# Moving turned tokens inside SBUF, and gathering the rows of five chunks by six transfers: a fused convolution and feed-forward kernel on one Trainium2 core

## The chip, the core and the metric

The kernel runs on one core of a Trainium2 chip. The metric is the device time of one execution in microseconds (us); below it stands as the median of three runs. The engines are TensorE (PE for the matmuls, PEld for the weight loads), VectorE (DVE), ScalarE (ACT), GpSimd (POOL) and SyncE (SP). SP computes nothing here: it issues transfers (DMAs), in the order in which they stand in its queue. SBUF is the core's working memory with 128 partitions; PSUM takes the matmuls' sums; DRAM is the large memory outside.

## The reference, cut to what matters

```python
# x: (8, 4096, 192), weight_gen: (8, 4096, 8 heads, 7 taps), all float32
w = softmax(weight_gen, over the 7 taps)
x_pad = 6 zero rows in front of every sequence of x
conv[b, s, h, g] = sum_k w[b, s, h, k] * x_pad[b, s + k, h, g]     # 24 channels a head
h = conv.reshape(32768, 192) @ w_in          # w_in: (192, 2048)
r = relu(h)
out = (r * r) @ w_out                        # w_out: (2048, 192)
```

## The kernel before

**Tiles.** Partition `p` holds 256 consecutive tokens. The program walks 64 chunks `c` of 4 tokens a partition, so a chunk has 512 tokens (`N`). For a chunk DVE computes the softmax and the convolution, token on partition, into a tile `pr` of 128 x 4 x 192 (line 392 multiplies by a tap, line 405 adds). The first product needs the channels on partitions: `turn` brings the chunk into `xT` (128 partitions x 3 x 512). There the 192 channels are three groups `k` of 64, and both halves of the partitions hold the same three groups, since two matmuls of 64 rows run side by side. ACT rounds `xT` to the high part `xh` (line 435) and DVE takes the rest as low part `xl` (line 438): three instructions each for a chunk, one for each `k`.

**The turn before.** VectorE's transpose (line 497) turns blocks of 32 x 32 into a tile `xr`. Four transfers (line 503) write `xr` to a tile `xd` in DRAM, and two (line 508) read `xd` back, one into each half of `xT`. SP issues the reads when all four writes have landed.

**The steps.** A chunk is 8 steps `j`. In a step PE runs 18 matmuls of the first product for chunk `c` (line 532), then the second product of a step two behind (lines 613 to 623, or 648). ACT runs ReLU, square and the rounding to `gh` (lines 549, 556, 560), DVE the difference `gl` or `du` (lines 569, 572). All other work is hung into these steps by a table (`at(chunk, step, function)`): the turn for chunk m stands at step 2 of chunk m - 1 (most m), the high parts at its steps 5 and 6, the low parts at 6 and 7.

**Two kinds of chunk.** Chunks 6 to 62 are scaled (`is_scaled`): their second product runs partly in fp16, with factors that `measure` takes from a group's input (ACT, line 270, at step 2 of an even chunk, two chunks ahead). Chunks 1 to 5 are not, and 0 and 63 go paths of their own.

**The output of a chunk.** PE leaves the result channel-major. `sum_turned` adds the two halves of the sums into a tile `X`; the 64 last channels also need the other half of the partitions added. `store_turned` transposes `X` by blocks into `Y` (lines 676 and 680) and gathers the rows token-major into `o_sb`. A scaled chunk does that by six transfers (line 686) and is written a step group later (`close_scaled`, line 697). An unscaled chunk adds the other half by a transfer on SP (line 664) and a DVE addition (line 679), gathers by 24 transfers of 16 KB (line 690), and is written at once by four transfers (line 102).

**SP's queue.** The next input group, `wt` and `xt` (lines 156 and 157, two chunks' worth), is loaded at step 5 of odd chunks, and so stands in SP's queue behind what `store_turned` issued at steps 3 and 4.

Of the kernel before, what the change touches and what calls it, by code (L numbers as in the profile page):

```python
# [8 lines left out]
F32 = mybir.dt.float32  # L9
# [5 lines left out]
ALU = mybir.AluOpType  # L15
# [15 lines left out]
def kernel(  # L31
# [9 lines left out]
    nc = tc.nc  # L41
    B, S, D = x.shape
# [3 lines left out]
    P = 128  # L46
    Q = 32
    HALO = K - 1
    R = B * S // P
    PPB = S // R  # L50
    TC = 4
    NCH = n_chunks or R // TC
# [3 lines left out]
    D1 = 64  # L56
    ND = D // D1
    N = TC * P
# [3 lines left out]
    N_PE = 2  # L62
# [7 lines left out]
    FIRST = 6  # L70
    GL_POOL = 5
    SCALE_STEP = NJ
# [8 lines left out]
    op = ctx.enter_context(tc.tile_pool(name="op", bufs=1))  # L81
    dram = ctx.enter_context(tc.tile_pool(name="dram", bufs=2, space=bass.MemoryType.DRAM))
# [6 lines left out]
    def put_out(c, t0, t1, o_sb, reads):  # L89
        rows = slice(rows_of(c) + t0, rows_of(c) + t1)  # L90
        if reads == 0:
            nc.sync.dma_start(out=out.rearrange("(p r) d -> p r d", r=R)[:, rows, :], in_=o_sb[:, t0:t1])
            return
        if reads == 3:
            v = out.rearrange("(q a b r) d -> b q a r d", q=P // Q, a=P // Q, r=R)
            n = v.shape[0] // 4
            for k in range(4):
                nc.sync.dma_start(out=v[k * n:(k + 1) * n, :, :, rows, :], in_=o_sb[k * Q:(k + 1) * Q, t0:t1])
            return
        v = out.rearrange("(q a b r) d -> q b a r d", q=P // Q, a=2 ** reads, r=R)  # L100
        for q in range(P // Q):
            nc.sync.dma_start(out=v[q, :, :, rows, :], in_=o_sb[q * Q:(q + 1) * Q, t0:t1])
# [7 lines left out]
    def is_scaled(c):  # L110
        return FIRST <= c < NCH - 1
# [21 lines left out]
    def rows_of(c):  # L133
        return (c + CPG if c < CPG else c - CPG if c < 2 * CPG else c) * TC
# [144 lines left out]
    def factor(gi):  # L279
        f = att.tile([P, 1], F32, name="x_fac", bufs=2)  # L280
        x_out[gi] = fo = att.tile([P, 1], F32, name="x_out", bufs=3)
        nc.vector.tensor_tensor(out=f, in0=x_pow[gi], in1=v_unroot, op=ALU.mult)  # L282
        n = P // (P // Q) ** 2
        for b in range(n):
            nc.gpsimd.dma_start(out=fo[b * P // n:(b + 1) * P // n], in_=f[b::n])  # L285
# [48 lines left out]
    def conv_steps(c, on_pe, moving=False):  # L334
# [3 lines left out]
        n = TC * H  # L338
        wf = wt[:, lo:lo + TC].rearrange("p t h k -> p (t h) k")
        if c < N_PE:  # L340
            e = eps[c]
# [5 lines left out]
        parts = xts[c] = {}  # L347
# [26 lines left out]
        prs = {}  # L374
# [115 lines left out]
        def turn():  # L490
            xr = att.tile([P, D // Q, P], F32, name="xr")
            xT = att.tile([P, ND, N], F32, name="xT")
            for k in range(ND):
                src[k] = xT[:, k]
            pr = prs.pop(0).rearrange("p t (b i) -> p t b i", i=Q)
            if c < NCH - 1:
                nc.vector.transpose(xr.rearrange("p b (t j) -> p t b j", j=Q), pr)
            else:
                for t in range(TC):
                    nc.vector.transpose(xr[:, :, t * Q:(t + 1) * Q].rearrange("p b (i m) -> p b m i", i=2), pr[:, t])  # L500
            xd = dram.tile([D, N], F32, name="xd")
            for q in range(P // Q):
                nc.sync.dma_start(
                    out=xd[:, q * P:(q + 1) * P].rearrange("(b i) n -> i b n", i=Q),
                    in_=xr[q * Q:(q + 1) * Q],
                )
            for h in range(2):
                nc.sync.dma_start(out=xT[h * D1:(h + 1) * D1], in_=xd.rearrange("(k p) n -> p k n", p=D1))

        return steps + taps() + [turn], splits  # L510

# [140 lines left out]
    def sum_turned(c, parts=(1, 0)):  # L652
        acc = accs[c]
        if c not in works:
            works[c] = stage.tile([P, 3, N], F32, name="raw")
        X = works[c]
        for k in parts:
            nc.scalar.copy(X[:, k], acc[2 * k])  # L658
        for k in parts:
            nc.vector.tensor_tensor(out=X[:, k], in0=acc[2 * k + 1], in1=X[:, k], op=ALU.add)  # L660
        if 1 in parts and is_scaled(c):
            nc.gpsimd.dma_start(out=X[0:D1, 1], in_=X[D1:P, 1], accum_op=ALU.add)  # L662
        elif 1 in parts:
            nc.sync.dma_start(out=X[0:D1, 2], in_=X[D1:P, 1])

    def store_turned(c, part):
        X = works[c]

        def blocks(v):
            return v.rearrange("p (a t i) -> p t a i", a=P // Q, t=TC) if is_scaled(c) else v  # L670

        if part == 0:
            o_sb = op.tile([P, TC, D], F32, name="o_sb", bufs=2)
            Y = stage.tile([P, 2, N], F32, name="raw")
            outs[c] = o_sb, Y
            nc.vector.transpose(blocks(Y[:, 0]), X[:, 0])
        else:
            if not is_scaled(c):
                nc.vector.tensor_tensor(out=X[0:D1, 1], in0=X[0:D1, 1], in1=X[0:D1, 2], op=ALU.add)
            nc.vector.transpose(blocks(outs[c][1][0:D1, 1]), X[0:D1, 1])  # L680
        o_sb, Y = outs[c]
        y = Y[:, part].rearrange("p (t q i) -> p q t i" if c < N_PE or is_scaled(c) else "p (q t i) -> p q t i", t=TC, i=Q)
        for e in range(P // Q if part == 0 else D1 // Q):
            d0 = part * P + e * Q
            if is_scaled(c):
                nc.sync.dma_start(out=o_sb[:, :, d0:d0 + Q], in_=outs[c][1][e * Q:(e + 1) * Q, part])
                continue
            for q in range(P // Q):
                queue = nc.gpsimd if part and c == NCH - 2 else nc.sync
                queue.dma_start(  # L690
                    out=o_sb[q * Q:(q + 1) * Q, :, d0:d0 + Q],
                    in_=y[e * Q:(e + 1) * Q, q],
                )
        if part and not is_scaled(c):
            put_out(c, 0, TC, o_sb, 2)

    def close_scaled(c):
        o_sb, f = outs[c][0], x_out[c // CPG]
        nc.vector.tensor_scalar(out=o_sb, in0=o_sb, scalar1=f, scalar2=f, op0=ALU.mult, op1=ALU.mult)
        put_out(c, 0, TC, o_sb, 3)  # L700

    outs = {}
# [19 lines left out]
    def store(c, t0, t1):  # L722
        put_out(c, t0, t1, outs[c][0], 1 if c == 0 else 0)
# [115 lines left out]
    def at(c, j, f):  # L839
        todo.setdefault((c + j // NJ, j % NJ), []).append(f)  # L840
# [40 lines left out]
    for gi in range(FIRST // CPG, NCH // CPG):  # L881
        at(CPG * gi - 2, 2, lambda gi=gi: measure(gi))
        at(CPG * gi - 2, 3, lambda gi=gi: power(gi))
        at(CPG * gi, 2, lambda gi=gi: factor(gi))
    for c in range(FIRST, NCH - 2):
        at(c + 1, SCALE_STEP, lambda c=c: close_scaled(c))

    plan_conv(2, conv2[6:], split2)
    plan_conv(3, *conv_steps(3, 0, True))
# [8 lines left out]
    for c in range(1, NCH):  # L898
        tail = c == NCH - 1
        for j in range(NJ):  # L900
# [28 lines left out]
            if split_sum:  # L929
                for f in fs[:N_AHEAD]:  # L930
                    f()
                del fs[:N_AHEAD]
                sum_turned(done, (0,))
            elif done is not None:
                sum_turned(done)
            if split_sum:
                highs_of(c, fbs)
                sum_turned(done, (1,))
            for f in fs:
                f()  # L940
            if c > 1:
                for part in range(2):
                    if j == (LOAD_STEP if tail else 2 * part + 2 if is_scaled(c - 1) else OUT_STEP + part):
                        store_turned(c - 1, part)
# [7 lines left out]
    c = NCH - 1  # L952
# [15 lines left out]
    t, end = TC - 1, range(NF - 4, NF)  # L968
# [6 lines left out]
    o_sb, tmp = outs[c]  # L975
# [33 lines left out]
```

## Time and profile before

| | |
|---|---|
| median of 3 runs | 2075.03 us (2075.01 to 2076.12) |
| the profiled execution's own time | 2076.22 us |
| span of its instructions | 2074.1 us, 1.00 of the full TensorE clock granted on average (0.998) |
| PE busy | 2054.8 us (99%) |
| DVE busy | 1873.6 us (90%) |
| ACT busy | 1840.6 us (89%) |
| POOL busy | 222.2 us (11%) |
| share of the chain that ended last | PE 84%, ACT 5%, DMA 3%, DVE 3% |
| transfers: hardware queue | 300280 packets, 181.04 MB, 37.6% of 16 engines |

The table is read so: the profiled execution's time lies 2.1 us over its span, and 1.2 us over the median. PE is nearly always busy, so the question for any change is what makes PE wait in the 1% that is left, and what makes its matmuls run at a lower clock.

### The profile page before, as it was taken

Reading aid. Unit: us, or ns where it says so; the run is one execution under the profiler, and the core shown is the slowest. Engines: PE = TensorE matmul, PEld = TensorE weight load, DVE = VectorE, ACT = ScalarE, POOL = GpSimd, SP = SyncE. Lnnn points to the kernel's source line nnn. Section 1 sums busy time; section 2 is a strip of 40 time slices with the busy share of each in tenths; the row PEclk is TensorE's granted clock in tenths of the full one; section 3 lists DMA queues with packets and bytes.
Section 4 is the critical chain, followed back from the end, with each engine's and each line's share of the span. In section 5 each row is a group of like instructions: output and inputs, shape, how many; then the busy total and the mean of one; then the engine's idle time right before and its main releaser. Section 6 shows DMA issues by size and latency. Waiting matters only on the chain.

```text
span 2074.1 us, 49551 instructions
## 1 busy us (share of the span) xinstructions
PE 2054.8 (99%) x19484; PEld 1621.0 (78%) x19484; DVE 1873.6 (90%) x2953; ACT 1840.6 (89%) x3551; POOL 222.2 (11%) x366
## 2 busy tenths in 40 slices
PE   9999999999999999999999999999999999999999
PEld 8898877777777777777777777777777777777778
DVE  8998989999999989999899998999989989999985
ACT  8988988989989989889898898998888988889986
POOL 0000110111110111101111101111011111011110
PEclk9999999999999999999999999999999999999999
DMA  8434454544544535545345454455453553544532
GB/s 233 95 64 100 109 123 97 119 84 100 122 106 107 120 66 117 117 101 119 74 108 125 98 113 92 94 119 115 100 118 72 112 127 95 114 86 100 121 61 56
DMA packets 322081, 217.78 MB, mean 105 GB/s; under 512 B 215584, under 2 KB 272928, under 8 KB 318008
## 3 DMA queue, kind: packets, MB, share of 16 engines
q1 hardware_dynamic: 300280, 181.04, 37.6%
q0 software_dynamic: 21568, 33.59, 9.6%
q8 instruction: 152, 2.49, 0.5%
q14 instruction: 81, 0.66, 0.1%
HBM read 106.52 MB, written 49.55 MB: 75 GB/s over the span
## 4 chain that ended last, share of the span: by engine, by line
PE 84%; ACT 5%; DMA 3%; DVE 3%; issue 1%; SPq 1%; POOL 0%; ACTq 0%; DVEq 0%; POOLq 0%
PE ph L532 42%; PE acc L613 25%; PE acc L617 9%; PE acc L623 5%; PE acc L648 3%; DMA xT<-xd 2%; ACT gh L560 1%; ACT rg L549 1%; ACT rg L556 1%; SPq L690 1%; PE acc L590 1%; DVE du L569 1%; DMA xt<-in_x_dram 1%; DMA pr<-pr 0%; ACT du L270 0%
## 5 line engine op out<-in xcount | busy, mean ns | idle before, releaser
L532 PE MATMUL ph<-xh,W 64*128 64x512 f32 x6096 | 909.5, 403 | 0.1
L549 ACT ACTIVATE rg<-ph 128x512 f32<-128x512 f32 x992 | 539.7, 598 | 174.3 <-PE ph L532 172.1
L532 PEld LDWEIGHTS ph<-xh,W 64*128 64x128 f32 x6096 | 578.5, 186 | 135.6 <-ACT gh L560 23.4
L613 PE MATMUL acc<-gh,V 64*128 64x512 f32 x5472 | 666.7, 376 | 0.0
L556 ACT ACTIVATE rg<-rg 128x512 f32<-128x512 f32 x1007 | 581.6, 636 | 0.2
L560 ACT CAST gh<-rg 128x512 fp32r<-128x512 f32 x1008 | 576.8, 628 | 3.0 <-PE acc L590 3.0
L613 PEld LDWEIGHTS acc<-gh,V 64*128 64x128 f32 x5472 | 519.6, 186 | 72.5 <-ACT gh L560 0.2
L532 PE MATMUL ph<-xl,W 64*128 64x512 f32 x3048 | 418.1, 377 | 9.7 <-DVE xl L438 9.3
L569 DVE TENSOR_TENSOR gl<-rg,gh 128x512 f16<-128x512 f32 x570 | 391.1, 742 | 31.7 <-ACT gh L560 31.7
L392 DVE TENSOR_TENSOR pr<-xt,wt 128x768 f32<-128x768 f32 x440 | 412.6, 950 | 2.5 <-DMA pr<-pr 0.2
L532 PEld LDWEIGHTS ph<-xl,W 64*128 64x128 f32 x3048 | 291.5, 186 | 54.7 <-DVE xl L438 15.0
L405 DVE TENSOR_TENSOR pr<-pr 128x768 f32<-128x768 f32 x309 | 294.8, 954 | 4.2
L569 DVE TENSOR_TENSOR du<-rg,gh 128x512 f16<-128x512 f32 x342 | 231.8, 732 | 48.6 <-ACT gh L560 48.4
L617 PE MATMUL acc<-gl,du 64*128 64x512 f16 x1140 | 173.4, 381 | 0.3 <-DVE gl L569 0.2
L662 POOL DMA_DIRECT2D raw<-raw x57 | 47.4, 831 | 1154.0 <-DVE raw L660 874.9
L660 DVE TENSOR_TENSOR raw<-acc,raw 128x512 f32<-128x512 f32 x124 | 85.3, 691 | 72.4 <-ACT raw L658 71.7
L617 PEld LDWEIGHTS <-du 64*128 64x128 f16 x1824 | 53.6, 95 | 109.9 <-issue 109.5
L435 ACT CAST xh<-xT 128x512 fp32r<-128x512 f32 x186 | 108.4, 619 | 26.1 <-DMA xT<-xd 25.9
L438 DVE TENSOR_TENSOR xl<-xT,xh 128x512 fp32r<-128x512 f32 x186 | 121.0, 681 | 2.3 <-ACT xh L435 2.3
L285 POOL DMA_DIRECT2D x_out<-x_fac x232 | 112.4, 494 | 85.6 <-DVE x_fac L282 82.2
L410 POOL DMA_DIRECT2D pr<-pr x63 | 56.7, 900 | 504.1 <-DVE pr L392 459.5
L617 PE MATMUL acc<-du 64*128 64x512 f16 x684 | 103.7, 382 | 0.0
(131 smaller groups left out, 1239.6 us busy)
## 6 DMA issues: line engine op xcount, KB each, us to landing
xT<-xd SPq DMA_DIRECT2D x124, 384.0 KB
xt<-in_x_dram SPq DMA_DIRECT2D x30, 1344.0 KB
out_dram<-o_sb SPq DMA_DIRECT2D x254, 96.0 KB
pr<-pr POOLq DMA_DIRECT2D x63, 384.0 KB, 5.9
xd<-xr SPq DMA_DIRECT2D x248, 96.0 KB
o_sb<-raw SPq DMA_DIRECT2D x342, 64.0 KB
raw<-raw POOLq DMA_DIRECT2D x57, 128.0 KB, 4.3
wt<-in_weight_gen_dram SPq DMA_DIRECT2D x31, 224.0 KB
```

The source lines that it names most:

```text
L285: nc.gpsimd.dma_start(out=fo[b * P // n:(b + 1) * P // n], in_=f[b::n])
L392: tt(out=dst, in0=src, in1=wf[:, t0 * H:t1 * H, k:k + 1].broadcast_to([P, m, G]), op=ALU.mult)
L405: tt(out=prs[k0], in0=prs[k0], in1=prs.pop(k), op=ALU.add)
L435: nc.scalar.copy(parts["h"][:, k, n], src[k][:, n])
L438: tt(out=parts["l"][:, k, n], in0=src[k][:, n], in1=parts["h"][:, k, n].bitcast(F32), op=ALU.subtract)
L532: nc.tensor.matmul(two[i], w, order(xx[rows, k]), start=(n == 0), stop=(n == last))
L549: nc.scalar.activation(r, ph, AF.Relu)
L556: nc.scalar.activation(r, r, AF.Square)
L560: nc.scalar.copy(gh, rgs[c, fb])
L569: nc.vector.tensor_tensor(out=gl, in0=g, in1=h, op=ALU.subtract)
L613: nc.tensor.matmul(acc[b + h], V[rows, fb, e:e + P], two_halves(g[rows]), start=fb == 0 and e < 2 * P, stop=False)
L617: nc.tensor.matmul(acc[h], V16[rows, 2 * j + i, 0:P], gls[c, j][rows, i], start=False, stop=last and i == 1)
```

## The change

`turn` no longer uses DRAM. The channels are taken in another order: two transposes, one for the even and one for the odd channels (`s`), each read `pr` with a step of two elements and write 384 contiguous elements. In `xr` a partition then holds what two neighbouring partitions of `xT` need, and eight transfers from SBUF to SBUF (for each quarter `q` of the source partitions, one into each half of `xT`) do the rest. `xT` is the same as before.

The unscaled chunks 1 to 5 take the path of the scaled ones: the other half is added by an accumulating transfer on POOL's queue, the transpose reads `X` in an order that leaves six gathers instead of 24, and `close` writes the chunk at step 0 of the chunk after (`at(c + 1, 8)`).

```diff
         if reads == 3: ...
+        if reads == 2:
+            v = out.rearrange("(q j r) d -> j q r d", q=P // Q, r=R)
+            n = Q // 4
+            for k in range(4):
+                nc.sync.dma_start(out=v[k * n:(k + 1) * n, :, rows, :], in_=o_sb[k * Q:(k + 1) * Q, t0:t1])
+            return
...
-            pr = prs.pop(0).rearrange("p t (b i) -> p t b i", i=Q)
+            pr = prs.pop(0).rearrange("p t (k i s) -> p s k t i", k=ND, s=2)
             if c < NCH - 1:
-                nc.vector.transpose(xr.rearrange("p b (t j) -> p t b j", j=Q), pr)
+                for s in range(2):
+                    nc.vector.transpose(xr[:, s * ND:(s + 1) * ND].rearrange("p k (t j) -> p k t j", j=Q), pr[:, s])
...
-            xd = dram.tile([D, N], F32, name="xd")
             for q in range(P // Q):
-                nc.sync.dma_start(
-                    out=xd[:, q * P:(q + 1) * P].rearrange("(b i) n -> i b n", i=Q),
-                    in_=xr[q * Q:(q + 1) * Q],
-                )
-            for h in range(2):
-                nc.sync.dma_start(out=xT[h * D1:(h + 1) * D1], in_=xd.rearrange("(k p) n -> p k n", p=D1))
+                for h in range(2):
+                    nc.sync.dma_start(out=xT[h * D1:(h + 1) * D1, :, q * P:(q + 1) * P], in_=xr[q * Q:(q + 1) * Q])
...
-        if 1 in parts and is_scaled(c):
+        if 1 in parts:
             nc.gpsimd.dma_start(out=X[0:D1, 1], in_=X[D1:P, 1], accum_op=ALU.add)
-        elif 1 in parts:
-            nc.sync.dma_start(out=X[0:D1, 2], in_=X[D1:P, 1])
...
+        x, y = X[0:n, part], Y[0:n, part]
+        if is_scaled(c):
+            nc.vector.transpose(y.rearrange("p (a t i) -> p t a i", a=P // Q, t=TC), x)
+        else:
+            y = y.rearrange("p (a t i) -> p t a i", a=P // Q, t=TC) if c < N_PE else y.rearrange("p (b i) -> p b i", i=Q)
+            nc.vector.transpose(y, x.rearrange("p (b m a) -> p b a m", a=4, m=Q // 4))
+        for e in range(n // Q):
             d0 = part * P + e * Q
-            for q in range(P // Q): ...
+            nc.sync.dma_start(out=o_sb[:, :, d0:d0 + Q], in_=Y[e * Q:(e + 1) * Q, part])
+
+    def close(c):
+        put_out(c, 0, TC, outs[c][0], 2)
...
-    for c in range(FIRST, NCH - 2):
-        at(c + 1, SCALE_STEP, lambda c=c: close_scaled(c))
+    for c in range(1, NCH - 2):
+        at(c + 1, SCALE_STEP, lambda c=c: (close_scaled if is_scaled(c) else close)(c))
```

On SP's queue this is what stands for chunks 2 to 4, before (`raw` is `X` or `Y`, an `x24` at the end counts transfers in a row):

```order
L664 DMA raw<-raw 64x512
L503 DMA xd<-xr 32x6x128 x4
L508 DMA xT<-xd 64x3x512 x2
L690 DMA o_sb<-raw 32x4x32 x24
L102 DMA out_dram<-o_sb 8x4x768 x4
L156 DMA wt<-in_weight_gen_dram 128x448
L157 DMA xt<-in_x_dram 128x2688
L664 DMA raw<-raw 64x512
```

And the same place now:

```order
L510 DMA xT<-xr 64x3x128 x8
L682 DMA o_sb<-raw 128x4x32 x6
L162 DMA wt<-in_weight_gen_dram 128x448
L163 DMA xt<-in_x_dram 128x2688
L104 DMA out_dram<-o_sb 8x4x768 x4
L510 DMA xT<-xr 64x3x128 x8
```

The input load now stands behind 8 + 6 transfers, no longer behind 4 + 2 + 24 + 4, and the chunk's four writes come after it.

On DVE at the turn of a scaled chunk, before (`raw` is the output's `Y` and `X`, `gl` the difference that the second product needs):

```order
L569 TENSOR_TENSOR gl<-rg,gh 128x2x256 x2
L282 TENSOR_TENSOR x_fac<-x_pow,coef 128x1
L497 STREAM_TRANSPOSE xr<-pr 128x4x6x32
L676 STREAM_TRANSPOSE raw<-raw 128x4x4x32
L569 TENSOR_TENSOR gl<-rg,gh 128x2x256 x2
```

And now:

```order
L571 TENSOR_TENSOR gl<-rg,gh 128x2x256 x2
L288 TENSOR_TENSOR x_fac<-x_pow,coef 128x1
L504 STREAM_TRANSPOSE xr<-pr 128x384 x2
L676 STREAM_TRANSPOSE raw<-raw 128x4x4x32
L571 TENSOR_TENSOR gl<-rg,gh 128x2x256 x2
```

One transpose of 768 elements a partition has become two of 384 in the same place; nothing else has moved there.

## Rows read from the trace of the kernel before

**Rows 1.** The page: busy time, share of the span and instructions of each engine.

```profile
PE 2054.8 (99%) x19484; PEld 1621.0 (78%) x19484; DVE 1873.6 (90%) x2953; ACT 1840.6 (89%) x3551; POOL 222.2 (11%) x366
```

**Rows 2.** Waits: who waited for whom, us in total, times, longest us.

```profile
ACT xh L435 <- DMA xT<-xd: 25.9, 34, 2.7
ACT du L270 <- DMA xt<-in_x_dram: 7.2, 2, 5.4
```

**Rows 3.** The chain that ended last: start us, us, what.

```profile
326.21 2.14 PE ph L532 x18
...
960.70 2.14 PE ph L532 x18
992.22 2.18 PE ph L532 x18
...
1025.40 2.14 PE ph L532 x18
...
2009.37 2.14 PE ph L532 x18
```

**Rows 4.** Timeline of a chunk whose turn is late: start us, us, engine, instructions [idle before].

```profile
997.38 1.83 SPq L503 DMA_DIRECT2D xd<-xr  x4
1002.66 1.30 SPq L508 DMA_DIRECT2D xT<-xd  x2
1009.77 1.14 ACT L435 CAST xh<-xT 128x512 fp32r<-128x512 f32 x2 [2.21 <-DMA xT<-xd]
```

**Rows 5.** Timeline of a chunk in which nobody waits for the turn.

```profile
1061.09 0.98 DVE L497 STREAM_TRANSPOSE xr<-pr 128x768 f32<-128x768 f32 x1
1062.10 1.81 SPq L503 DMA_DIRECT2D xd<-xr  x4
1063.50 1.39 DVE L569 TENSOR_TENSOR gl<-rg,gh 128x512 f16<-128x512 f32 x2 [0.83 <-ACT gh L560]
1065.73 1.29 SPq L508 DMA_DIRECT2D xT<-xd  x2
1072.24 1.15 ACT L435 CAST xh<-xT 128x512 fp32r<-128x512 f32 x2
```

**Rows 6.** DMA view of two stretches: packets, MB, share of 16 engines (1062 to 1065.8, 1002.6 to 1006.9).

```profile
q1 hardware_dynamic: 832, 0.39, 50.9%
...
q1 hardware_dynamic: 306, 0.59, 55.6%
```

**Rows 7.** Timeline of chunks 3 and 4: SP, ACT and PE.

```profile
139.08 16.75 SPq L690 DMA_DIRECT2D o_sb<-raw  x24
159.54 0.42 SPq L157 DMA_DIRECT2D xt<-in_x_dram  x1
166.61 1.48 ACT L270 ACTIVATE du<-xt 128x1536 bf16<-128x1536 f32 x1 [5.38 <-DMA xt<-in_x_dram]
156.97 0.83 PE L532 MATMUL ph<-xh,W 64*128 64x512 f32 x6
161.07 0.83 PE L532 MATMUL ph<-xh,W 64*128 64x512 f32 x6
174.77 0.81 PE L532 MATMUL ph<-xh,W 64*128 64x512 f32 x6
```

**Rows 8.** Busy time of the engines from 170 to 174.5; behind POOL the granted clock.

```profile
170.00:174.50 4.50, 3.95 (x18) 3.01 (x20) 4.00 (x11) 4.50 (x10) 0.00 (x0) 0.62 0.50 108
```

**Rows 9.** Timeline of chunk 6: ACT and PE.

```profile
234.92 1.49 ACT L270 ACTIVATE du<-xt 128x1536 bf16<-128x1536 f32 x1 [1.83 <-DMA xt<-in_x_dram]
254.76 0.48 PE L532 MATMUL ph<-xl,W 64*128 64x512 f32 x2 [2.07 <-DVE xl L438]
```

**Rows 10.** Groups by line, shapes kept apart: count | busy us, mean ns | idle before.

```profile
L497 DVE STREAM_TRANSPOSE xr<-pr 128x768 f32<-128x768 f32 x61 | 59.5, 975 | 0.1
L500 DVE STREAM_TRANSPOSE xr<-pr 128x192 f32<-128x192 f32 x4 | 1.5, 499 | 0.0
L226 DVE SCALAR_TENSOR_TENSOR du<-raw,du 128x384 uint32<-128x384 uint32 x16 | 8.6, 554 | 0.0
```

More of the change, by code (lines that the diff above doesn't have):

```diff
@@ L494, in turn @@
                 src[k] = xT[:, k]
-            pr = prs.pop(0).rearrange("p t (b i) -> p t b i", i=Q)
+            pr = prs.pop(0).rearrange("p t (k i s) -> p s k t i", k=ND, s=2)
             if c < NCH - 1:
-                nc.vector.transpose(xr.rearrange("p b (t j) -> p t b j", j=Q), pr)
+                for s in range(2):
+                    nc.vector.transpose(xr[:, s * ND:(s + 1) * ND].rearrange("p k (t j) -> p k t j", j=Q), pr[:, s])
             else:
                 for t in range(TC):
-                    nc.vector.transpose(xr[:, :, t * Q:(t + 1) * Q].rearrange("p b (i m) -> p b m i", i=2), pr[:, t])
-            xd = dram.tile([D, N], F32, name="xd")
+                    nc.vector.transpose(xr[:, :, t * Q:(t + 1) * Q].rearrange("p b (i m) -> p b m i", i=2), pr[:, :, :, t])
             for q in range(P // Q):
-                nc.sync.dma_start(
-                    out=xd[:, q * P:(q + 1) * P].rearrange("(b i) n -> i b n", i=Q),
-                    in_=xr[q * Q:(q + 1) * Q],
-                )
-            for h in range(2):
-                nc.sync.dma_start(out=xT[h * D1:(h + 1) * D1], in_=xd.rearrange("(k p) n -> p k n", p=D1))
+                for h in range(2):
+                    nc.sync.dma_start(out=xT[h * D1:(h + 1) * D1, :, q * P:(q + 1) * P], in_=xr[q * Q:(q + 1) * Q])
         return steps + taps() + [turn], splits
@@ L660, in sum_turned @@
             nc.vector.tensor_tensor(out=X[:, k], in0=acc[2 * k + 1], in1=X[:, k], op=ALU.add)
-        if 1 in parts and is_scaled(c):
+        if 1 in parts:
             nc.gpsimd.dma_start(out=X[0:D1, 1], in_=X[D1:P, 1], accum_op=ALU.add)
-        elif 1 in parts:
-            nc.sync.dma_start(out=X[0:D1, 2], in_=X[D1:P, 1])
     def store_turned(c, part):
         X = works[c]
-        def blocks(v):
-            return v.rearrange("p (a t i) -> p t a i", a=P // Q, t=TC) if is_scaled(c) else v
+        n = D1 if part else P
         if part == 0:
@@ L675, in store_turned @@
             outs[c] = o_sb, Y
-            nc.vector.transpose(blocks(Y[:, 0]), X[:, 0])
-        else:
[L678 to L683, printed above, removed]
-            d0 = part * P + e * Q
[L685 to L695, printed above, removed]
+        o_sb, Y = outs[c]
+        x, y = X[0:n, part], Y[0:n, part]
+        if is_scaled(c):
+            nc.vector.transpose(y.rearrange("p (a t i) -> p t a i", a=P // Q, t=TC), x)
+        else:
+            y = y.rearrange("p (a t i) -> p t a i", a=P // Q, t=TC) if c < N_PE else y.rearrange("p (b i) -> p b i", i=Q)
+            nc.vector.transpose(y, x.rearrange("p (b m a) -> p b a m", a=4, m=Q // 4))
+        for e in range(n // Q):
+            d0 = part * P + e * Q
+            nc.sync.dma_start(out=o_sb[:, :, d0:d0 + Q], in_=Y[e * Q:(e + 1) * Q, part])
+    def close(c):
+        put_out(c, 0, TC, outs[c][0], 2)
     def close_scaled(c):
```

## The prediction, on record before the changed kernel ran

> **What bounds the kernel now.** I read the page first: PE is busy for 2054.8 us, 99% of the span [rows 1], so only what makes PE wait or run slowly can be won. Next, who waited for whom. Two waits for transfers stand out, both on ACT: 34 times, 25.9 us in all and 2.7 us at the longest, for `xT`, the turned tokens, and twice, 7.2 us in all, for the input load `xt` [rows 2].
>
> What they cost PE is read from the chain that ended last [rows 3]. The 18 matmuls that begin a chunk's last step recur at 960.70 and 992.22, which makes an undisturbed chunk 31.52 us, and then at 1025.40, which makes the next 33.18. From 326.21 to 2009.37 are 53 chunks: 1683.16 us, where 53 x 31.52 is 1670.56. **In the steady part 12.6 us are lost**, and all else there is PE at its own pace.
>
> Why the chunk before 1025.40 lost 1.66 is in its timeline [rows 4]. SP issued the four writes to `xd` at 997.38, could issue the reads only at 1002.66, and ACT sat idle for 2.21 us until `xT` landed at 1009.77. So about 0.55 us of such a wait is absorbed and the rest goes to PE. The undisturbed chunk [rows 5] shows how near that always is: the transpose ended at 1062.07 (1061.09 + 0.98), and ACT took `xT` at 1072.24 without waiting. ACT therefore wants `xT` **10.17 us after the transpose**; in the late chunk it came 12.4 us after SP could begin.
>
> The early part loses in another way [rows 7]. In chunk 3 SP spends 16.75 us on 24 gathers, from 139.08, then writes the chunk, and issues the load of `xt` only at 159.54. ACT needs it for `measure` and idles 5.38 us until 166.61. PE's first-product groups start at 156.97 and 161.07, 4.10 us for a step; the one two steps on starts at 174.77, 13.70 us later where 8.20 are due: 5.5 us lost. That is more than a wait, since after PE's idle stretch the granted clock was 0.62 on average from 170 to 174.5 [rows 8], part of it at the lower of the two levels, 1.2 GHz instead of 2.4. In chunk 6 the same load is 1.83 us late, and PE later idles 2.07 us for a low part `xl` that DVE, set back with ACT, brings late [rows 9].
>
> **The turn, part by part.** Removed: four writes to DRAM, the wait for them, two reads. Added: eight transfers of 96 KB, 64 x 3 runs of 512 bytes each, and one transpose more.
>
> When will `xT` land? Issue first. Before, four transfers of the same 192 runs took 1.81 us of SP, a pitch of 0.45, and SP saw the last of them landed at 1065.73, which is 3.63 us after the first issue and 2.27 after the fourth one's (1062.10 + 3 x 0.45) [rows 5]. Eight at that pitch land 7 x 0.45 + 2.27 = 5.4 us after the transpose. If each takes as long to issue as a read does (1.29 / 2 = 0.65 us), it is 6.8. Then the data. The packets of the writes were 832, all but 64 of 512 bytes, with 50.9% of 16 engines over 3.8 us: 37 ns each. Eight transfers have 1536 such packets, 3.6 us on 16 engines, which hides under the issuing. No row shows a plain 512-byte packet from SBUF to SBUF; the upper bound is a 2 KB packet from DRAM, 55.6% of 16 engines over 4.3 us for 306, so 125 ns [rows 6], and with it the data alone take 12 us. I take 37 ns, the same size and source, and so a landing at 5.4 to 6.8 us. Now and then a transfer is held up: in the late chunk SP waited 5.28 us after the first issue instead of 3.63 [rows 4, 5]. With that 1.65 on top it is 8.5 at worst, still before 10.17. **All of the 12.6 us should go.** Behind the eight on SP stand the chunk's six gathers, which nobody needs before the next chunk; they could begin at 1067.02 (1065.73 + 1.29), 4.95 us after the transpose, and now can after eight issues, 3.6 to 5.2 us after it.
>
> The transposes. One of 768 elements took 975 ns; two of 384 that read with a step of two elements are not in the trace. From below they cost the same; an elementwise instruction that reads one operand with that step took 554 ns for 384 [rows 10], and two such are 1.11 us, 0.13 more. From above: the last chunk's transposes, which write with a long step, took 499 ns for 192 elements, 2.6 ns each, so 2.0 us and 1.02 more. I take 0.13, the row with the same step on the same side. What hides it is the 0.83 us for which DVE then waits for ACT's `gh` [rows 5]. At the upper bound 0.2 us would spill into a DVE that has no gap for the next 20 us, and the `xl` at its end would be 0.2 us later; PE would feel little of it. Cost: nothing, 0 to 0.2 us a chunk.
>
> The Trainium skill has a rule against this part. DMA: Bandwidth & Descriptors, section Rules for kernel authors, advises one large transfer instead of many small ones, and calls transfers to disjoint halves of the partitions not worth while because they share the same 16 engines. By that page's fit (section Anatomy of one DMA, about 2.0 us plus the bytes at 436 GB/s), eight in a row without overlap would be an estimated 17.8 us, and the change a loss. The trace disagrees on the overlap: four transfers landed within 3.63 us of the first issue [rows 5].
>
> **The output of chunks 1 to 5.** Removed: 24 gathers in favour of six, DVE's addition, SP's `raw` transfer. The load of `xt` now stands behind eight and six transfers; six at 0.70 (16.75 / 24) are 4.2 us, so at chunk 3 it leaves SP near 145 instead of 159.54, some 14 us earlier, more than the 5.38 it was late; likewise for the 1.83 at chunk 6. That returns 5.5 us and, by the gap alone, 2.07. The accumulating transfer goes to POOL, which is 11% busy [rows 1], steps ahead of its use. The ten transposes that read `X` with a step of four cost DVE between nothing and 0.7 us each (the 1.02 above, at 512 instead of 768 elements); the removed addition makes up for part of it, and PE's late `xl` in chunk 6 is the place where it could show.
>
> **The sum**, against the profiled execution's own 2076.2 us: 12.6 + 5.5 + 2.07 = 20.2 us, so 2056.0. That execution ran 1.2 us over the median of the runs, 2075.03, so for the median I predict **2055 us**, 1.0% faster.
>
> **Rivals.**
> - *Only the turn pays.* The early stalls stay, because something else is late next: ACT has much extra work in chunks 4 to 6, so that without the load's wait it may still set PE back, or the strided transposes keep DVE late. For it: PE's gap in chunk 6 was for DVE, not for the load. Against it: in chunk 4 the idle ACT waited for nothing but the load. Time: 2075.0 - 12.6 = 2062.4, with the half of it gone 2058.6.
> - *The wait is replaced.* `xT` comes early, but the third `xl` of a chunk is then held by DVE itself, which runs without a gap from 1063.50. Against it: undisturbed chunks run at 31.52 us with that same DVE. Time: within 2 us of 2075.
> - *Slower: the eight transfers do not overlap.* They land when the engines have worked off 1536 packets. At 125 ns that is 12 us of data and, with 1.6 us for first and last, 13.6; ACT then waits 3.4 us in each of some 60 chunks and PE loses 2.9: 170 us, a time near 2245. It turns into a loss as soon as they land about 10.7 us after the transpose. In a row without overlap, 8 x 2.27 = 18.2 us, it would be some 450. Against it: 37 ns for the same size, and the four overlapped.
>
> **How the numbers follow.** Forecast, all or nearly all waits gone: 0.68, 2052 to 2058 (below the sum, because chunk 6's loss may be more than its gap). Only the turn, or the turn and half of the rest: 0.19, 2058 to 2066. Replaced: 0.06. Slower: 0.04. The last 0.03 is a gain larger than I can see. The range takes in the first two cases: 2050 to 2066. About 0.2%, 4 us, is what a measurement of this kernel can tell from no change. Faster by more than that: 0.68 + 0.19 + 0.03 = 0.90; same 0.06; slower 0.04.
>
> **What would show it.** Right: ACT's wait for `xT` is gone from the list of waits; eight transfers on SP take 3.6 to 5.5 us, and `xh` follows without idling; the chain's starts keep 31.52 us from chunk 8 to the end; the load in chunk 3 leaves SP near 145; no stretch at a lower clock between the first chunk and the last. Wrong: transposes of well over 2 us for a chunk; an idle ACT before `xh`; DVE or ACT as the releaser of PE every chunk; a load of `xt` still late in chunk 4.

## The result, and the profile after

The changed kernel takes **2058.05 us** (median of 4 runs, 2057.33 to 2058.45) where the kernel before takes 2075.57 (4 runs, 2075.01 to 2077.0): a ratio of 0.9914, 95% interval 0.9897 to 0.9931, or 17.5 us less. The forecast was 2055, with a range of 2050 to 2066.

The page of the changed kernel, busy time by engine and traffic:

```profile
PE 2046.7 (100%) x19484; PEld 1619.0 (79%) x19484; DVE 1884.8 (92%) x3009; ACT 1839.8 (90%) x3551; POOL 226.2 (11%) x371
HBM read 57.77 MB, written 25.17 MB: 40 GB/s over the span
```

PE is busy for 8 us less than in [rows 1] with the same 19484 matmuls. In the list of waits, ACT's two lines of [rows 2] have no counterpart left: ACT does not wait for `xT`, and `measure` does not wait for `xt`. Of the waits of PE and its weight loads for an `xl`, the longest that are left are these (us, times, longest):

```profile
PEld ph L534 <- DVE xl L444: 2.5, 2, 2.2
...
PE ph L534 <- DVE xl L444: 1.8, 1, 1.8
```

The chain that ended last, at the same steps as [rows 3] (start us, us, what). These are the third steps of their chunks, right behind the end of the second product of the chunk before, and not the last steps as the prediction has it; the sums do not depend on the name:

```profile
319.99 2.14 PE ph L534 x18
...
981.94 2.14 PE ph L534 x18
...
1013.46 2.14 PE ph L534 x18
...
1044.99 2.14 PE ph L534 x18
...
1990.63 2.14 PE ph L534 x18
```

From 319.99 to 1990.63 are the same 53 chunks: 1670.64 us, where 53 x 31.52 is 1670.56. The steady part loses nothing any more; before it lost 12.6. The first of these starts comes 6.2 us earlier than its 326.21 of before: that is what the early part gave, with 0.5 of it there before chunk 1 (its first product starts at 52.83 instead of 53.36). 12.5 + 6.2 = 18.7, and the span fell by 18.5, from 2074.1 to 2055.6.

A steady chunk in its timeline, the counterpart of [rows 5] (the fence takes DVE, SP and ACT together):

```profile
1080.62 1.27 DVE L504 STREAM_TRANSPOSE xr<-pr 128x384 f32<-128x384 f32 x2
1081.96 5.87 SPq L510 DMA_DIRECT2D xT<-xr  x8
1087.92 5.18 SPq L682 DMA_DIRECT2D o_sb<-raw  x5
1091.74 1.13 ACT L441 CAST xh<-xT 128x512 fp32r<-128x512 f32 x2
```

The eight transfers follow the transposes at once, there is no second issue that waits for a first, and ACT takes `xT` 9.85 us after the transposes' end (1091.74 - 1081.89) without idling. Chunk 3 and chunk 6, the counterparts of [rows 7] and [rows 9]:

```profile
138.69 4.04 SPq L682 DMA_DIRECT2D o_sb<-raw  x6
...
143.44 0.69 SPq L163 DMA_DIRECT2D xt<-in_x_dram  x1
...
161.31 1.48 ACT L276 ACTIVATE du<-xt 128x1536 bf16<-128x1536 f32 x1
...
234.84 1.28 DVE L679 STREAM_TRANSPOSE raw<-raw 128x512 f32<-128x512 f32 x1
...
238.11 1.25 DVE L679 STREAM_TRANSPOSE raw<-raw 64x512 f32<-64x512 f32 x1
...
247.81 0.68 DVE L444 TENSOR_TENSOR xl<-xT,xh 128x512 fp32r<-128x512 f32 x1
...
248.54 0.48 PE L534 MATMUL ph<-xl,W 64*128 64x512 f32 x2 [1.78 <-DVE xl L444]
```

Six gathers take 4.04 us instead of 16.75, the load of `xt` leaves SP at 143.44 instead of 159.54, and ACT starts `measure` at 161.31 with no idle time ahead of it. But PE still idles 1.78 us for `xl`, and DVE, which brings it, works without a pause from 223.9 on: the two transposes of chunk 5's store now cost it 1.28 and 1.25. (DVE makes this `xl` in its work of chunk 6, which is why the prediction and the expectations speak of chunk 6; on PE the idle time lies in the first step of chunk 7, which is the first to need it.) The groups, and the granted clock (behind POOL, 1.00) from 251 to 2016:

```profile
L504 DVE STREAM_TRANSPOSE xr<-pr 128x384 f32<-128x384 f32 x122 | 74.8, 662 | 0.1
L676 DVE STREAM_TRANSPOSE raw<-raw 64x512 f32<-64x512 f32 x57 | 39.8, 698 | 0.0
L676 DVE STREAM_TRANSPOSE raw<-raw 128x512 f32<-128x512 f32 x57 | 39.1, 686 | 0.0
L679 DVE STREAM_TRANSPOSE raw<-raw 128x512 f32<-128x512 f32 x5 | 5.8, 1162 | 0.0
L679 DVE STREAM_TRANSPOSE raw<-raw 64x512 f32<-64x512 f32 x5 | 5.7, 1147 | 0.0
```

```profile
251.00:2016.00 1765.00, 1765.00 (x17024) 1367.93 (x17020) 1625.84 (x2562) 1593.23 (x3077) 203.62 (x334) 1.00 0.42 92
```

### The profile page after: what moved, and what is told of

It is laid out like the page before. It is cut to its first block, busy times and chain, and to the rows that moved or that the text cites. A ratio compares the mean times of both kernels' runs of the same rounds, so it can differ in the third digit from the quotient of the medians.

```text
span 2055.6 us, 49787 instructions
## 1 busy us (share of the span) xinstructions
PE 2046.7 (100%) x19484; PEld 1619.0 (79%) x19484; DVE 1884.8 (92%) x3009; ACT 1839.8 (90%) x3551; POOL 226.2 (11%) x371
## 3 DMA queue, kind: packets, MB, share of 16 engines
q0 software_dynamic: 21968, 34.25, 10.2%
## 4 chain that ended last, share of the span: by engine, by line
PE 91%; DVE 5%; issue 1%; ACT 1%; DMA 1%; DVEq 0%; SPq 0%; POOLq 0%
PE ph L534 45%; PE acc L615 28%; PE acc L619 10%; PE acc L625 5%; PE acc L650 2%; DVE gl L574 1%; DVE pr L411 1%; PE acc L592 1%; DVE pr L398 1%; DMA pr<-pr 1%; DVE raw L679 0%; DVE xr L504 0%; DVE gl L571 0%; DVE xl L444 0%; ACT rg L558 0%
```

## The experiments

The theory to be tested: the turn pays because `xT` lands before ACT wants it, and the output pays because the load of `xt` comes to its turn earlier on SP. The rivals: the lighter traffic pays, or the gathers and DVE's addition as such. Three groups of runs were made on three chips, each beside the kernel before; times are compared within a group, and where they are not, the text says so.

**One part alone.** The kernel before with only the new `turn`:

```
+ for s in range(2):
+     nc.vector.transpose(xr[:, s * ND:(s + 1) * ND]..., pr[:, s])
...
+ nc.sync.dma_start(out=xT[h * D1:(h + 1) * D1, :, q * P:(q + 1) * P], in_=xr[q * Q:(q + 1) * Q])
```

> The kernel before with the turn alone changed (two transposes, eight transfers inside SBUF); chunks 1 to 5 are stored as before, with 24 gathers. Theory (the turn pays by xT's landing, the output by the input load's place on SP, and the two add up): 12.4 us of waits and of half clock in the steady part go, the early loss stays: 2075.5 - 12.4 = 2063, ratio 0.994; ACT's waits for xT gone, its two waits for xt (7.2 us) still there, chunk starts 31.52 us apart from chunk 8 on. Rival (the two parts need each other): more than 2066 or less than 2060.

And with only the new store of chunks 1 to 5 (`put_out` with reads == 2, `close`, six gathers):

> The kernel before with the output of chunks 1 to 5 alone changed (six gathers, written a step later); the turn goes through DRAM. Theory: only the early part gains, 5 to 6 us: 2070, ratio 0.9973; ACT's waits for xt gone, some 34 waits for xT of about 26 us still there, and 12 us of steady loss. Rival (it is the lighter load on the DMA engines that pays): the waits for xT shrink as well in the chunks after the fifth, which this edit does not touch, and the time falls below 2066.

Measured, with 2072.37 us for before (18 runs): the turn alone 2064.61 (0.9959, interval 0.9947 to 0.9972), the output alone 2067.75 (0.9977, 0.9966 to 0.9988). ACT's waits for `xT` and `xt`, first with the turn alone, then with the output alone:

```profile
ACT du L270 <- DMA xt<-in_x_dram: 8.3, 2, 5.3
```

```profile
ACT xh L441 <- DMA xT<-xd: 24.5, 27, 2.5
```

Each part takes away its own wait and leaves the other's. The lighter load on the DMA engines by the output did nothing for `xT` in later chunks: ACT waits for it 27 times, as often as in the run below that keeps all 24 gathers (27 times, 22.9 us). As sums the two give -7.8 and -4.6 against 2072.4, 12.4 in all; the whole change gave 17.5 and, in the second group, 18.7. The sum falls short by 5 to 6 us, of which some 3 lie in the time before, which was lower in this group. Where the rest lies the chains show, first with the turn alone (and ACT's second wait for `xt` in that run), then with the output alone:

```profile
327.67 2.14 PE ph L528 x18
...
1998.84 2.14 PE ph L528 x18
234.72 1.49 ACT L270 ACTIVATE du<-xt 128x1536 bf16<-128x1536 f32 x1 [3.07 <-DMA xt<-in_x_dram]
```

```profile
319.12 2.14 PE ph L538 x18
...
2000.13 2.14 PE ph L538 x18
```

The 53 steady chunks lose 0.6 us with the turn alone (1671.17 - 1670.56) and 10.4 with the output alone. But with the turn alone the way from chunk 1's first product to the first of these starts is 275.4 us (327.67 - 52.30), 2.5 longer than the 272.85 of before (326.21 - 53.36): the second wait for `xt` is 3.07 us instead of 1.83, PE then idles 2.21 us for `xl`, and the granted clock is 0.83 from 252 to 262. With the output alone that way is 267.3 us, 5.6 shorter. So the turn gives its 12 us in the steady part and the output its 5.6 in the early part, and the turn alone gives some 2.5 back, which the whole change does not.

**The same order without new transfers.** The kernel before, the turn one step earlier but still through DRAM:

```
- SCALED_SLOTS = (2, 1, 4, 1, 3, 1, 2, 2, 2, 1)
+ SCALED_SLOTS = (2, 1, 4, 1, 3, 1, 2, 2, 3)
```

> The kernel before with the turn of chunks 6 to 62 begun one step (about 4 us) earlier, still by four writes to DRAM and two reads. Theory (only the moment at which xT lands counts, not where the bytes go): every wait for xT is at most 2.7 us and xT now has about 4 us more, so the waits and the 12.4 us go: 2063, ratio 0.994, with HBM traffic as before (106 MB read). Rival 1 (the traffic through DRAM itself costs the time): 2075, no change. Rival 2 (the transposes one step earlier hold DVE at another place, the wait is replaced): 2070 or more, with PE waiting for xl or gl.

The kernel before, the load of `xt` ahead of the 24 gathers:

```
- if j == (LOAD_STEP if c > 1 else 0) and c % 2 ...
+ if j == ((LOAD_STEP if c > 5 else 3) if c > 1 else 0) and c % 2 ...
```

> The kernel before with the load of xt in chunks 3 and 5 put into step 3, ahead of the 24 gathers on SP; all transfers are as many as before. Theory (the early loss is the load's place in SP's line): ACT's wait of 5.38 us for xt is gone, PE gains at least the 5.5 us of chunk 4: 2070 or a little less, ratio 0.997. Rival (it is DVE's and SP's own work on 24 gathers and the addition that costs): 2074 to 2076.

Measured: 2064.04 (0.9957, interval 0.9945 to 0.997), as much as the SBUF turn; and 2067.40 (0.9975, 0.9966 to 0.9984), as much as the new output. With the early turn ACT's waits for `xT` come down to one, though the traffic is that of before (waits, and the page):

```profile
ACT xh L435 <- DMA xT<-xd: 0.7, 1, 0.7
```

```profile
HBM read 106.52 MB, written 49.55 MB: 76 GB/s over the span
```

With the load first, ACT starts `measure` in chunk 4 at once, while SP is as busy with 24 gathers as before (timeline):

```profile
138.80 0.43 SPq L157 DMA_DIRECT2D xt<-in_x_dram  x1
139.28 18.74 SPq L690 DMA_DIRECT2D o_sb<-raw  x24
...
160.23 1.48 ACT L270 ACTIVATE du<-xt 128x1536 bf16<-128x1536 f32 x1
```

Both rivals fall, as far as these times can tell: neither DRAM traffic nor the number of gathers is what cost the time; it is when two transfers land. In the run with the early turn, ACT's two waits for `xt` stay, as they must, and PE lost 2.1 us in one steady chunk, near 1451, where DVE waited 2.39 us for an accumulating transfer on POOL's queue; what held that transfer is not settled.

**The whole change again, and both orders together.** In the second group, with 2074.99 us for before (11 runs, 2070.43 to 2080.63):

> The changed kernel once more, beside the kernels of this group on one chip. Theory (both parts add up, on each chip against its own time before): the turn alone gave -7.8 us and the output alone -4.6 where the time before was 2072.4, so about -12.4 there, and -17.5 where it was 2075.6; the time after is near 2058 to 2060 on any chip, since no wait for a transfer is left in it. Rival (the gain itself depends on the chip): the ratio stays at 0.9914 whatever the time before, or the time after moves with it.

> The kernel before with two orders changed and no transfer: the turn of chunks 6 to 62 one step earlier, still through DRAM, and the load of xt in chunks 3 and 5 ahead of the 24 gathers. Theory (only the times at which xT and xt land count): -8.3 and -5.0 add up to -13 us against its own before, equal to the changed kernel within 2 us, so 2058 to 2061. Rival (transfers inside SBUF or fewer gathers give something of their own): 3 us or more slower than the changed kernel.

The changed kernel took 2056.32 (0.991, interval 0.9896 to 0.9924; 5 runs, 2056.22 to 2056.48), the two orders alone 2055.54 (0.9909, 0.9895 to 0.9923). Both lie below what was expected, by 1.7 and 2.5 us. That the time after hardly moves (2058.05 and 2056.32) while that of before does (2072.0 to 2075.6 as medians of the groups) fits the theory, but this chip's time before was so near to that of the first comparison that the rival with its constant ratio is not told apart. And **two edited orders did as much as moving the tokens inside SBUF**, with all DRAM traffic and, in chunks 1 to 5, the 24 gathers a chunk kept. In the waits of that run:

```profile
ACT xh L435 <- DMA xT<-xd: 0.8, 1, 0.8
```

**What is left of the early loss.** In the changed kernel the steps of chunks 3 and 4 that start at 115.31, 136.03 and 169.47 take 4.33, 4.72 and 4.56 us instead of 4.10, together 1.3 too much, and the step that ends at 251.06, the first of chunk 7, takes 5.90 instead of 3.68, 2.2 too much. Two edits, in the second group:

```
- nc.vector.transpose(y, x.rearrange("p (b m a) -> p b a m", a=4, m=Q // 4))
+ nc.vector.transpose(y, x.rearrange("p (b i) -> p b i", i=Q))
```

> The changed kernel with the transposes of the stores of chunks 1 to 5 reading X without the step of four; the rows of these chunks then stand in another order within blocks of 32 in the output. Theory (the strided transposes hold DVE, which keeps the low part xl late in chunk 6): a store takes 1.4 us of DVE instead of 2.3, PE's gap of 1.78 us before chunk 6's last step falls to about 0.85, and the whole is 1 to 1.5 us faster than the changed kernel. Rival (the gap has another cause): gap and time unchanged within 0.3 us.

```
- ... else OUT_STEP + part):
+ ... else NJ - 1 if c == FIRST else OUT_STEP + part):
...
+ at(c + 1, SCALE_STEP + (c == FIRST - 1), ...close...)
```

> The changed kernel with chunk 5's two store transposes put into the last step of chunk 6, behind the low parts xl, and its output written one step later. Theory: the 2.3 us of transposes no longer stand before xl on DVE, PE's gap of 1.78 us goes, and the time falls by 1.5 to 2.2 us. Rival (the wait only moves): DVE, now 2.3 us late after xl, holds PE in chunk 7 or 8 instead, time as that of the changed kernel within 0.5 us.

Measured: 2054.34 (5 runs, 2053.99 to 2057.87) and 2055.25 (6 runs, 2054.91 to 2056.89), beside 2056.32. The first leaves out the right order of the rows, so it only tells what the step of four costs. In it the transposes take 0.70 us (the groups), and PE's gap falls to 0.60 (the timeline):

```profile
L679 DVE STREAM_TRANSPOSE raw<-raw 128x512 f32<-128x512 f32 x5 | 3.5, 704 | 0.0
L679 DVE STREAM_TRANSPOSE raw<-raw 64x512 f32<-64x512 f32 x5 | 3.5, 699 | 0.0
```

```profile
249.09 0.48 PE L534 MATMUL ph<-xl,W 64*128 64x512 f32 x2 [0.60 <-DVE xl L444]
```

In the second the gap falls to 0.32, and no later chunk pays for it: the chunk starts stay 31.52 apart. Its 1.1 us are less than the 1.5 to 2.2 expected. The step that lost 2.2 us loses 1.05 in the first run and 0.76 in the second. So DVE was what held it, and the step of four in the transposes was about half of that. In the third group (before 2071.97, 7 runs) the plain transposes with the reordering put into the writes, and both edits together:

```
- v = out.rearrange("(q j r) d -> j q r d", q=P // Q, r=R)
+ v = out.rearrange("(q a b r) d -> b a q r d", q=P // Q, a=P // Q, r=R)
+ n = P // v.shape[0]
+ for k in range(v.shape[0]):
+     nc.sync.dma_start(out=v[k, :, :, rows, :], in_=o_sb[k * n:(k + 1) * n, t0:t1])
```

> The changed kernel with the transposes of the stores of chunks 1 to 5 read in plain order, and the reordering of rows put into the writes to the output instead: eight writes of 16 partitions for such a chunk in place of four of 32. Theory (DVE's 0.9 us a chunk is what counts, SP has room): 1.3 to 2.3 us faster than the changed kernel's 2056.3, as the run with rows in another order; steps at 115, 136 and 169 back to their usual length, PE's gap in chunk 6 under 1 us. Rival (four writes more on SP, 2.6 us a chunk, delay xT or xt in chunks 2 to 6): no gain, ACT waiting for xT or xt.

> Both edits of DVE's early work in one kernel: plain transposes in the stores of chunks 1 to 5 with eight writes, and chunk 5's store put behind the low parts in chunk 6. Theory: what is left of the early loss (about 1.3 us in chunks 3 to 5 and 2.2 in chunk 6) goes nearly whole: 2053 to 2054, 20 us or more below the kernel before. Rival (the last gap is ACT's or PE's, not DVE's): equal to the better of the two edits alone, 2054.3 to 2055.3.

Measured: 2054.02 (4 runs, 2053.64 to 2054.34) and **2053.35** (4 runs, 2053.31 to 2054.27), 0.9907 of before (0.9893 to 0.9922). The three long steps are back at 4.10 in both, and the first step of chunk 7 loses 1.1 and 0.8 us instead of 2.2. The last is the fastest kernel of this study by its median; it lies 18.6 us below the kernel before, not the 20 expected, since the kernel before was faster on this chip. The changed kernel was not run in this group. What can be compared across the chips is the way from chunk 1's first product to the third step of chunk 9 in the traces: 267.1 us in both traces of the changed kernel, and 264.5, 265.6, 264.7 and 264.3 in these four runs in the order told. The first edit in its right form thus gives the 2.4 us that the lengths of the steps promise (1.3 + 1.1). With the two orders alone that way takes 265.4: so the six gathers in place of 24 give nothing there that the strided transposes do not take back.

**How much time is in hand.** The turn one step later, in the changed kernel and in the kernel before, by the same edit:

```
- SCALED_SLOTS = (2, 1, 4, 1, 3, 1, 2, 2, 2, 1)
+ SCALED_SLOTS = (2, 1, 4, 1, 3, 1, 2, 2, 2, 0, 1)
```

> The changed kernel with the turn of chunks 6 to 62 begun one step (3.67 us) later. Theory (ACT takes xh 9.9 us after the transposes and the eight transfers land about 7.5 us after them, so the change has 2.4 us in hand): landing 11.2 us after the old moment, 1.3 us late, 0.55 of it absorbed, 0.75 us lost in each of 57 chunks: about 43 us, 2085 to 2115. Rival 1 (the transfers land far earlier than the packets say): within 5 us of 2056. Rival 2 (they land only just in time): 3.1 us lost a chunk, 2230.

> The kernel before with the same turn one step later, through DRAM. Theory: by that road xT lands about 9.7 us after the transpose, almost at the moment at which ACT wants it; 3.67 us later ACT waits some 3.2 us, PE loses 2.65 in each of 57 chunks: about 150 us, near 2225, and more where PE's idle time brings the lower clock (to 2330). The difference between this run and the one with eight transfers, over 57 chunks, is then how much earlier the eight land: about 2 us. Rival (both roads land at the same time and the gain is from traffic): the same loss for both within 30 us.

Measured, by two runs each: 2168.94 us (1.0464, interval 1.0441 to 1.0487) and 2331.88 (1.125, 1.121 to 1.129). Three late chunks of the first, in their timeline (DVE, SP, ACT):

```profile
1005.20 5.28 SPq L510 DMA_DIRECT2D xT<-xr  x8
1014.01 1.14 ACT L441 CAST xh<-xT 128x512 fp32r<-128x512 f32 x2 [1.15 <-DMA xT<-xr]
...
1037.99 1.23 DVE L504 STREAM_TRANSPOSE xr<-pr 128x384 f32<-128x384 f32 x2
1039.29 5.26 SPq L510 DMA_DIRECT2D xT<-xr  x8
1046.66 1.14 ACT L441 CAST xh<-xT 128x512 fp32r<-128x512 f32 x2 [1.66 <-DMA xT<-xr]
...
1137.64 1.12 DVE L504 STREAM_TRANSPOSE xr<-pr 128x384 f32<-128x384 f32 x2
1139.87 5.24 SPq L510 DMA_DIRECT2D xT<-xr  x8
1149.70 1.14 ACT L441 CAST xh<-xT 128x512 fp32r<-128x512 f32 x2 [3.09 <-DMA xT<-xr]
```

and the waits of the second, with PE's busy time in the first and in the second (the pages):

```profile
ACT xh L435 <- DMA xT<-xd: 276.5, 58, 8.4
PE 2075.1 (96%) x19484; PEld 1614.0 (75%) x19484; DVE 1889.1 (87%) x3009; ACT 1840.3 (85%) x3551; POOL 226.2 (10%) x371
PE 2132.1 (92%) x19484; PEld 1634.3 (70%) x19484; DVE 1877.2 (81%) x2953; ACT 1840.5 (79%) x3551; POOL 221.6 (10%) x366
```

Where ACT really waits, the landing of the eight is seen: 7.44 us after the transposes' end in one chunk (1046.66 - 1039.22), 10.9 in another (1149.70 - 1138.76). Over the 53 turns of chunks 6 to 62 in which ACT waits it lies between 7.4 and 11.1, with a median of 9.4. So against ACT's 9.85 the best landings leave 2.4 us in hand, and the slow ones of this run would leave nothing. In the changed kernel nobody waits, so no row shows its landing, only that it came in time in each chunk. The two runs are not alike in this: one step later, four gathers of the store stand ahead of the eight on SP, which in the changed kernel follow them. The expected 2085 to 2115 missed because it took 7.5 for every landing: 113 us more than 2056.3 (the second group's) is 2.0 a chunk, not 0.75. The gathers explain a part: in the chunk at 1137.64 SP was still issuing them when the transposes ended, and the eight began 1.1 us late. But there are chunks whose eight began at once and landed only after 10.6 us; what held those is open.

The run through DRAM took 163 us longer, a little more than the 2330 allowed for. Not all of that is landing: the same 19484 matmuls kept PE busy for 57 us more, at a mean granted clock of 0.979 against 0.998. With that and the 6 us of the early part taken off, some 100 us are left, 1.8 in each of 57 chunks. The landings themselves say the same: by DRAM `xT` came 9.6 to 14.4 us after the transpose, with a median of 11.4. So equal landings are refuted: started one step late, the eight land about 2 us earlier.

## Why the prediction was right, and where it was off

*What bounds the kernel* and *the steady part*: right. The 12.6 us were ACT's waits for `xT`, and 12.5 came back. The runs show the cause too: the waits go with the earlier landing, by either road, and grow when the turn starts later.

*The landing*: eight issues take 5.3 us in most chunks, a pitch of 0.66, which is the read's 0.65 and not the write's 0.45, and up to 6.6 in some. The landing, 5.4 to 6.8 forecast, was 7.4 at best where a run shows it, and up to 11.1 there. ACT's deadline of 10.17 holds for the kernel before; in the changed one it is 9.85, since the two transposes end 0.3 us later. The margin is 2.4 us at best instead of 3.4 to 4.8; it was enough in every chunk, but by how much in the slowest no run shows.

*The rule of the Trainium skill* against many small transfers (DMA: Bandwidth & Descriptors, section Rules for kernel authors): the 17.8 us for eight without overlap are not what the trace shows, 7.4 to 11.1. The fit behind them (section Anatomy of one DMA) is given there for transfers issued from GpSimd, while these eight go out on SP. The advice was no measure here, since one of two dependent stages went with the split. The slower rival, 2245 or more, falls with it.

*The transposes of the turn*: forecast at 0.13 us more a chunk, bound 1.02. Two of 662 ns against one of 975 are 0.35; PE felt nothing of it, as said.

*The early part*: **the mis-sized term.** 5.5 + 2.07 = 7.57 were forecast, 6.2 came, and of that about 0.5 stands already in the first chunk's start (PE begins the first products after the turn on PE at 52.83 instead of 53.36), which the change does not touch; over all runs that start lies between 51.8 and 56.0. The step that failed is "that returns 5.5 us and, by the gap alone, 2.07". The load of `xt` did come 16 us earlier and ACT's two waits went, and the 5.5 of chunk 4 came back, but the gap in chunk 6 belonged to DVE and only shrank from 2.07 to 1.78, and the three steps of chunks 3 and 4 that took 1.3 us too long were new for the most part. The prediction named that place, and left the price of the transposes with a step of four between nothing and 0.7 us; it is 0.48 (1162 against 686 ns) and 0.45 (1147 against 698). Taken off, they give 2.0 us back by the medians, 2.4 to 2.6 by the traces. So the rival "only the turn, or the turn and half of the rest" was half true: the early gain is three quarters of its term.

The rows give 2.27 ns an element with a step of four and 1.34 without. The Trainium skill has a note on lines of 16 bytes (SBUF — State Buffer, section Door 1: The DMA port swizzle). It says that an access which crosses to a new line pays a penalty, as each one does at a step of four fp32 elements, and the trace agrees; but it also says that one can stride four fp32 elements for free. There the trace disagrees for this instruction, and the measurement decides.

*From the profiled execution to the median*: the sum gave 2056.0 for the execution, which took 2057.33; 1.0 us was taken off for the median, and the median lies 0.7 above. The miss of 3.05 us is 1.33 + 1.0 + 0.7: more than half is the step from one execution to the median of a few.

## What to carry to other kernels

Before a route is rebuilt to be faster, ask how late its data are: where a transfer misses its reader by 1 to 3 us, moving its start by one step, or another queue entry out of its way, can give the whole gain; here two edited orders gave it. Read a deadline from a chunk that truly does not wait, and test the margin by starting later on purpose, looking at all the landings and not at one, and at what else then stands ahead in the queue. And when a wait goes, look at the engine behind it: DVE was next, and a transpose's read step decided about half of what was left.

## What was not expected of the hardware

- **The step at which a transpose reads costs, the partitions don't.** 128x512 in plain order 686 to 704 ns, with a step of four 1162; 64x512 with a step of four 1147. With a step of two, 662 ns for 384 elements (1.72 ns each) against 975 for 768 (1.27), but part of that is the shorter instruction: on the line through 692 ns for 512 elements and 975 for 768, 384 would take about 550, an estimate, so the step of two costs some 0.1 us.
- **The kernels in which ACT waits for `xT` scatter most.** The kernel before spreads over 5.6 to 10.2 us in the three groups (7 to 18 runs), the output alone over 7.6 (8 runs), the load first over 8.8 (11 runs). The kernels without these waits spread over 0.26 (the changed one, 5 runs) to 4.6 us. That the waits are the cause is not shown.
- **PE's idle time can cost more than itself, but not always.** In the run with the turn alone PE idled 2.91 us at 166.39; the clock was then at half (first row, behind POOL), that is 1.2 GHz, while PE was never idle in that stretch. In the changed kernel it idled 1.78 us at 246.76 and the clock stayed at 1.00 (second row):

```profile
169.30:172.50 3.20, 3.20 (x14) 2.32 (x16) 3.03 (x10) 3.20 (x7) 0.00 (x0) 0.50 0.75 149
```

```profile
246.80:251.00 4.20, 2.46 (x22) 1.93 (x24) 4.20 (x7) 3.13 (x7) 0.00 (x0) 1.00 0.17 69
```
